# Linear attention and a gated MLP on one core: first loads, GpSimd's constants and the opening matmuls rearranged

## The chip, the core and the metric

The kernel runs on one core of one Trainium2 chip. The core has five engines that run their own instruction streams and wait for each other by semaphores: TensorE (PE in the profile; its weight loads are PEld), VectorE (DVE), ScalarE (ACT), GpSimd (POOL) and SyncE (SP). Transfers between HBM and SBUF run on 16 DMA engines that all queues share. The metric is the device time of one execution in microseconds. Before the change it is 287.11 us (median of 6 runs, 286.8 to 287.7).

## The reference

```python
kv = np.einsum('bhsd,bhse->bhde', k, v)                # 8 batches, 8 heads, 576 rows, 64 columns
out = np.einsum('bhsd,bhde->bhse', q, kv)
rms = np.sqrt(np.mean(out * out, axis=-1, keepdims=True) + 1e-06)
x = (out / rms * g_norm)                               # -> 4608 tokens x 512 (8 heads x 64)
h = x @ w_in                                           # 512 x 2048
g = h * (1.0 / (1.0 + np.exp(-1.702 * h)))
return g @ w_out                                       # 2048 x 512, fp32
```

All inputs are fp32. There is no softmax: each head's 64 x 64 `kv` is formed from all its rows, then multiplied by q, normed, and the result of all heads is the input row of the MLP.

## The kernel before

**Tiles.** Heads are taken in four pairs of two (128 columns). The MLP runs over nine tiles of 512 tokens: tile t below 8 holds the first 512 rows of batch t, and tile 8 holds the 64 remaining rows of all eight batches. For a tile the MLP first makes the hidden values in 16 column blocks `fo` of 128 (`hT`, L438: four matmuls over the row blocks `ko` of w_in, then a gate on ScalarE, L447, into `gT`), then projects them (`o`, L475: 4 output blocks `mo` times 16 `fo`). Row block `ko` of w_in meets exactly head pair `ko` of x, so a matmul with `ko` = 3 needs the attention result of pair 3.

**Order.** The schedule is manual: each engine gets its instructions in the order in which the program writes them, and waits for what each one needs. The attention of batch t+1 is woven into the MLP of tile t: `units1` are called after column block `fo` of the first half, `units2` after step n of the projection's 64 steps. The lists in the main loop (`at1`, `at2`) are these places.

**Casting loads.** All arithmetic is in fp16, so most fp32 inputs are cast while they are loaded, and all such loads are issued from GpSimd. Its instructions and its DMA issues are one stream in program order. A load waits at issue, where needed, for the landing of the eighth load before it.

**The start.** Batch 0 (`First`) has nothing to be woven into. Pair 0's k, q and v are loaded as fp32 from SP (L147) and cast by VectorE and ScalarE (L553 to L555). GpSimd first sets the constants: `ident` (L152, for the transposes of q) and `ones2` (L161 to L163: a block mask for `kv`, and the weights of the row sums `ss`), and then issues the casting loads of pairs 1 to 3 (q, k, v of each), with w_in's first row block for columns 0 to 511 put between q and k of pair 3, and then the rest of w_in in seven pieces. TensorE starts with 64 matmuls of 64 columns and 4 of 512 on zeros, so that its clock is up when the data comes; `busy(n)` are more of these. Each pair then goes through `q` (transposes, L393, copied to `qT` by VectorE), `kv` (L376, masked into `kvb` by VectorE, L383), `out` (L259, squared by ScalarE into `sq`, L279), `sums` (`ss` L339 on TensorE, `ln` L341 on ScalarE), `rs` (L347, ScalarE) and `apply` (L353, VectorE, which writes the pair's rows of `xT`). `ss` is `sums` and `rs` in one. The call list from L571 on interleaves pairs, and puts the first w_in matmuls (`d0.mm(ko, fo)`) between them: row block 0 before `kv(3)`, row blocks 1 and 2 after it, of six column blocks in all (GROUP), and row block 3 of the six at the end.

**Behind it.** After the w_in loads GpSimd issues w_out in pieces and batch 1's q, k and v among them. The remaining rows of batch 0 (`out(NPAIR)`, four matmuls of 64 columns at L270) are called after column block 7 of tile 0. PSUM is in three pools: `ps_h` (3 buffers), `ps_a` (3) and `ps_o` (2); a tile waits until the one that had its buffer has been read.

## Time and profile before

| quantity | value |
|---|---|
| median of 6 runs | 287.11 us |
| the profiled execution's own time | 287.02 us |
| its span, first to last instruction | 285.3 us |
| TensorE busy | 277.9 us, 97% |
| ScalarE, VectorE, GpSimd busy | 156.0, 118.9, 59.8 us |
| granted TensorE clock, mean | 0.999 |
| casting queue (software_dynamic), whole span | 15.59 MB written, 33.8% of 16 engines |

A line of the timeline is: start, length, engine, source line, operation, what it writes and reads, count, and in brackets how long the engine sat idle before and what ended that. A line of the chain that ended last is: start, length, what. A line of the table by stage is: stretch, its length, busy time (and instructions) of PE, PEld, DVE, ACT and POOL, the granted clock, the transfers' busy share and the GB/s that they moved (counted in bytes written, so a casting load reads twice as much). Matmuls overlap, so the length of one (379 ns for 512 columns) is longer than the distance from start to start (216 ns).

### The profile page before, as it was taken

The page shows a single profiled execution, that of the slowest core. Times are in us where ns is not written, and L with a number is a line of the kernel's source. Part 1 is how long each engine was busy: PE and PEld are TensorE (multiplying, and loading weights), DVE is VectorE, ACT ScalarE, POOL GpSimd, SP SyncE. Part 2 cuts the span into 40 slices and gives each one's busy share as a digit, 9 for nine tenths or more (in the row PEclk, how much of TensorE's full clock was granted, in tenths as well). Part 3 has the DMA queues.
Part 4 walks back from the last instruction along what each step waited for, and adds up shares of the span by engine and source line. Part 5 has one row for each costly group of instructions (what it writes and reads, how often), then busy time and mean ns, then how long its engine had stood idle before and what let it go on. Part 6 is the DMA issues. An engine that isn't in the chain of part 4 may idle for free.

```text
span 285.3 us, 4458 instructions
## 1 busy us (share of the span) xinstructions
PE 277.9 (97%) x1768; PEld 136.8 (48%) x1768; DVE 118.9 (42%) x230; ACT 156.0 (55%) x273; POOL 59.8 (21%) x86
## 2 busy tenths in 40 slices
PE   7799999999999999999999999999999999999995
PEld 5334554455445544554455445544454444444443
DVE  2550557527661657147713852286327400110001
ACT  2688439766575645574468536763666365016400
POOL 8762372111211121112011401130001100000000
PEclk9999999999999999999999999999999999999999
DMA  8999999998579356953798278925401410012022
GB/s 180 176 199 205 205 224 256 240 247 152 125 163 256 66 133 171 243 90 64 223 206 145 40 211 214 174 38 184 85 0 37 118 68 0 2 62 85 0 74 75
DMA packets 55158, 38.78 MB, mean 136 GB/s; under 512 B 31282, under 2 KB 52018, under 8 KB 55010
## 3 DMA queue, kind: packets, MB, share of 16 engines
q0 software_dynamic: 16048, 15.59, 33.8%
q1 hardware_dynamic: 38688, 22.39, 30.1%
q10 hardware_dynamic: 402, 0.52, 0.5%
q8 instruction: 14, 0.23, 0.3%
q14 instruction: 6, 0.05, 0.1%
HBM read 36.73 MB, written 9.44 MB: 162 GB/s over the span
## 4 chain that ended last, share of the span: by engine, by line
PE 93%; DMA 2%; POOL 2%; ACT 1%; DVE 0%; issue 0%
PE hT L438 43%; PE o L475 42%; PE kvp L227 3%; DMA vbuf<-in_v_dram 2%; PE outR L291 2%; PE oh L507 1%; PE ss L339 1%; POOL qraw L91 1%; POOL kraw L91 1%; POOL vbuf L91 0%; PE q L416 0%; ACT sq L279 0%; PE outT L270 0%; PE outT L259 0%; ACT ln L341 0%; ACT rs L347 0%
## 5 line engine op out<-in xcount | busy, mean ns | idle before, releaser
L475 PE MATMUL o<-w_out_sb,gT 128*128 128x512 f16 x560 | 130.7, 379 | 0.0
L447 ACT ACTIVATE gT<-hT 128x512 f16<-128x512 f32 x144 | 84.5, 601 | 75.9 <-PE hT L438 75.8
L438 PE MATMUL hT<-xT,w_in_sb 128*128 128x512 f16 x512 | 116.5, 379 | 1.2 <-DMA w_in_sb<-in_moe_w_in_dram 1.2
L438 PEld LDWEIGHTS <-w_in_sb 128*128 128x128 f16 x576 | 54.5, 98 | 63.6 <-DMA w_in_sb<-in_moe_w_in_dram 1.8
L475 PEld LDWEIGHTS <-gT 128*128 128x128 f16 x560 | 52.9, 98 | 56.7 <-issue 0.4
L485 DVE COPY osb<-o 128x512 f32<-128x512 f32 x20 | 13.8, 690 | 62.4 <-PE o L475 62.4
L323 POOL TENSOR_TENSOR x<-xr,g_all 128x512 f16<-128x512 f32 x12 | 15.3, 1272 | 70.4 <-DVE xr L316 46.3
L218 DVE COPY kpad<-kraw 64x576 f16<-64x576 f16 x56 | 25.0, 446 | 1.3
L240 DVE CAST kvb<-kvp 64x128 f16<-64x128 f32 x28 | 8.1, 289 | 39.9 <-PE kvp L227 39.7
L302 DVE TENSOR_REDUCE sum<-sq 128x8 f32<-128x512 f16 x24 | 15.8, 679 | 19.1 <-ACT sq L299 19.1
L112 POOL DMA_DIRECT2D kraw<-in_k_dram x16 | 10.0, 628 | 50.5 <-DVE kpad L218 34.6
L316 DVE TENSOR_TENSOR xr<-outR,sum 128x512 f32<-128x512 f32 x24 | 15.5, 686 | 11.1 <-ACT sum L313 11.1
L112 POOL DMA_DIRECT2D vbuf<-in_v_dram x16 | 9.7, 610 | 31.7 <-PE kvp L227 28.1
L323 DVE TENSOR_TENSOR x<-xr,g_all 128x512 f16<-128x512 f32 x12 | 15.2, 1267 | 0.7
L299 ACT ACTIVATE sq<-outR 128x512 f16<-128x512 f32 x24 | 13.6, 590 | 2.0 <-PE outR L291 1.6
L279 ACT ACTIVATE sq<-outT 128x512 f16<-128x512 f32 (+1 forms) x16 | 7.7, 486 | 12.5 <-PE outT L259 11.1
L227 PEld LDWEIGHTS <-kpad 128*128 128x128 f16 x252 | 11.1, 98 | 6.4
L438 PE MATMUL hT<-x_rem,w_in_sb 128*128 128x512 f16 x64 | 14.0, 379 | 0.0
L485 ACT COPY osb<-o 128x512 f32<-128x512 f32 x15 | 8.7, 582 | 6.3 <-PE o L475 6.3
L227 PE MATMUL kvp<-vbuf,kpad 128*128 128x64 f16 x252 | 11.9, 193 | 0.0
L312 ACT ACTIVATE sum<-sum,eps_t 128x16 f32<-128x16 f32 x12 | 3.7, 308 | 15.0 <-DVE sum L302 14.9
L341 ACT ACTIVATE ln<-ss,eps_t 128x512 f32<-128x512 f32 (+1 forms) x16 | 9.4, 586 | 3.2 <-PE ss L339 3.1
(64 smaller groups left out, 143.8 us busy)
## 6 DMA issues: line engine op xcount, KB each, us to landing
qf<-in_q_dram SPq DMA_DIRECT2D x5, 1024.0 KB, 9.4
out_dram<-osb SPq DMA_DIRECT2D x10, 512.0 KB, 2.9
kraw<-in_k_dram POOLq DMA_DIRECT2D x12, 288.0 KB, 7.5
vbuf<-in_v_dram POOLq DMA_DIRECT2D x12, 288.0 KB, 5.5
out_dram<-osb SPq DMA_DIRECT2D x6, 192.0 KB, 5.8
w_in_sb<-in_moe_w_in_dram POOLq DMA_DIRECT2D x4, 256.0 KB, 8.2
w_out_sb<-in_moe_w_out_dram POOLq DMA_DIRECT2D x2, 512.0 KB, 14.0
w_out_sb<-in_moe_w_out_dram POOLq DMA_DIRECT2D x4, 256.0 KB, 10.2
```

Of the source, the lines that this page charges most:

```text
L112: nc.gpsimd.dma_start(out=raw[n][l * PH : (l + 1) * PH, c0:c1, 0 : NH * D], in_=srcs[n][b].rearrange("(c l) (p j) d -> l p c (j d)", l=2, ...
L218: nc.vector.tensor_copy(out=kpad[r, c, :, l * D : (l + 1) * D], in_=kraw[r, c, 0 : NH * D].rearrange("p (j d) -> p j d", j=NH),)
L227: nc.tensor.matmul(self.kvp[:, c, :], kpad[:, c, j, :], vbuf[:, c, j * D : (j + 1) * D], start=(j == 0), stop=(j == NH - 1),)
L299: nc.scalar.activation(sq, t, AFT.Square)
L302: nc.vector.tensor_reduce(out=self.sum2[:, j % 2, :], in_=sq.rearrange("p (h d) -> p h d", h=H), op=ALU.add, axis=mybir.AxisListType.X,)
L316: nc.vector.tensor_mul(xr[:, i], self.o[j + i].rearrange("p (h d) -> p h d", h=H), s2[:, i, :].unsqueeze(2).to_broadcast([P, H, D]),)
L323: (nc.vector if i else nc.gpsimd).tensor_mul(self.x16[:, j + i, :].rearrange("p (h d) -> p h d", h=H), xr[:, i], g_all.unsqueeze(1).to_bro ...
L341: nc.scalar.activation(ln[:, 0:n], t[:, 0:n], AFT.Ln, bias=eps_t, scale=1.0 / D)
L438: nc.tensor.matmul(self.h[fo], w_in_sb[:, ko, fo * P : (fo + 1) * P], self.x[:, ko], start=(ko == 0), stop=(ko == KO - 1),)
L447: nc.scalar.activation(self.gT[:, fo, :], self.h[fo], AFT.Gelu_apprx_sigmoid)
L475: nc.tensor.matmul(os[mo], gT[:, fo, mo * P : (mo + 1) * P], w_out_sb[:, fo, :], start=(fo == 0), stop=(fo == FO - 1),)
L485: copy(osb[:, mo, :], os[mo])
```

## The change

1. v of pair 0 is no longer an fp32 load from SP with a cast on VectorE. It is the first casting load of GpSimd, ahead of everything else there.
2. GpSimd issues q, k, v of pair 1 and q of pair 2 before it sets `ident` and `ones2`. k and v of pair 2 and all of pair 3 follow.
3. w_in's first piece isn't put among pair 3's loads. After v of pair 3 come row blocks 0 and 1 in one load, then 2 and 3, then columns 4–5, 6–9 and 10–15: five loads instead of eight.
4. TensorE's opening is three fp32 matmuls of 512 columns on a new tile `zeros`, in place of 64 of 64 columns and 4 of 512.
5. In the call list, `kv(3)` and `out(3)` come before the first w_in matmul. The w_in matmuls then run in the order of `ko`: four column blocks each, `ss(3)` after the third of `ko` 0, and the column blocks 4 and 5 after all four of the first four.
6. The loads of w_out and of batch 1 are regrouped, batch 1's units sit at other steps, the order of column blocks at the head of tile 1 is 0, 1, 2, 3, batch 2's kv runs one column block sooner, and tile 7's output is stored in two halves.

```diff
     first = {}
-    for n in "kqv":
+    early_load("v", 0, 0, 1)
+    for n in "kq":
         first[n] = stage.tile([P, H, J * D], F32, name=f"{n}f", tag=f"{n}f")
...
+    zeros = const.tile([P, SM], F32)
+    nc.vector.memset(zeros, 0.0)
     nc.vector.memset(kvb[1], 0.0)
...
+    for n in "qkv":
+        early_load(n, 0, 1, 2)
+    early_load("q", 0, 2, 3)
     nc.gpsimd.affine_select(
...
-    for c in range(1, NPAIR):
-        for n in "qkv":
+    for c in range(2, NPAIR):
+        for n in "qkv"[c == 2 :]:
             early_load(n, 0, c, c + 1)
-            if c == NPAIR - 1 and n == "q":
-                load_w_in(0, 4, 0, 1)
-    load_w_in(0, 4, 1, 2)
+    load_w_in(0, 4, 0, 2)
     load_w_in(0, 4, 2, KO)
     load_w_in(4, GROUP)
-    load_w_in(GROUP, 8)
-    load_w_in(8, 10)
-    load_w_in(10, 13)
-    load_w_in(13, FO)
+    load_w_in(GROUP, 10)
+    load_w_in(10, FO)
...
-            order = [(ko, fo) for part in ((0, 3, 1, 2), range(4, group)) for ko in (0, 1) for fo in part]
+            order = [(ko, fo) for part in (range(4), range(4, group)) for ko in (0, 1) for fo in part]
...
-    nc.vector.tensor_copy(vbuf[0:PE_, 0, :], first["v"])
...
-    for _ in range(64):
-        nc.tensor.matmul(
-            idle_ps[:, 0:D], kvb[1][:, 0, :], kvb[1][:, 0, 0:D], start=True, stop=True
-        )
-    busy(4)
+    for _ in range(3):
+        nc.tensor.matmul(idle_ps, zeros[:, 0:P], zeros, start=True, stop=True)
...
     a0.q(3)
+    a0.kv(3)
+    a0.sums(2)
     a0.apply(1)
+    a0.out(3)
+    a0.rs(2)
+    a0.apply(2)
+    busy(1)
     d0 = Hidden(0)
-    d0.mm(0, 0)
-    a0.sums(2)
-    a0.rs(2)
-    d0.mm(0, 1)
-    d0.mm(0, 2)
-    d0.mm(0, 3, ps_a, "att")
-    a0.kv(3)
-    a0.apply(2)
-    a0.out(3)
     for fo in range(4):
-        d0.mm(1, fo)
+        d0.mm(0, fo, *((ps_h, "hT") if fo < 3 else (ps_a, "att")))
         if fo == 2:
             a0.ss(3)
             a0.apply(3)
-    for fo in range(4):
-        d0.mm(2, fo)
+    for ko in range(1, KO):
+        for fo in range(4):
+            d0.mm(ko, fo)
     for fo in range(4, GROUP):
-        for ko in range(KO - 1):
+        for ko in range(KO):
             d0.mm(ko, fo, ps_o, "o")
-    for fo in range(GROUP):
-        d0.mm(KO - 1, fo)
...
-    load_half("k", 1, 0, 2)
-    load_w_out(8, 10)
-    load_w_out(10, 12)
-    load_half("v", 1, 0, 2)
-    load_half("k", 1, 2, NPAIR)
-    load_half("v", 1, 2, NPAIR)
-    load_w_out(12, 14)
-    load_w_out(14, FO)
+    for c in (0, 2):
+        load_half("k", 1, c, c + 2)
+        load_half("v", 1, c, c + 2)
+        if c == 0:
+            load_w_out(8, 12)
+        else:
+            load_w_out(12, 14)
+            load_w_out(14, FO)
...
-    HALVED = (2, 3, 4, 5, 6)
+    HALVED = (2, 3, 4, 5, 6, 7)
...
-                at2((21, 21, 38, 38)[c], of(1, "pack_k", c))
-                at2((36, 37, 46, 47)[c], of(1, "kv", c))
-                o = (41, 43, 52, 53)[c]
+                at2((21, 21, 33, 33)[c], of(1, "pack_k", c))
+                at2((27, 28, 42, 43)[c], of(1, "kv", c))
+                o = (32, 35, 50, 53)[c]
                 at2(o, of(1, "out", c))
                 if c == NPAIR - 1:
-                    at2(48, load_kv, 2)
-                at2((45, 48, 56, 58)[c], of(1, "ss", c))
-                at2((48, 51, 56, 60)[c], of(1, "apply", c))
+                    at2(46, load_kv, 2)
+                at2((38, 46, 56, 59)[c], of(1, "ss", c))
+                at2((38, 46, 56, 59)[c], of(1, "apply", c))
...
-                at1(12 if t == 1 else f0, load_q, t + 2)
-                at1((11 if t == 1 else 9) + 4, load_kv, t + 2)
+                at1(f0, load_q, t + 2)
+                at1((10 if t == 1 else 9) + 4, load_kv, t + 2)
             for c in range(NPAIR):
                 at1(f0, of(b, "pack_k", c))
-                at1((11 if t == 1 else 9) + c, of(b, "kv", c))
+                at1((10 if t == 1 else 9) + c, of(b, "kv", c))
```

## The prediction

> **What bounds the kernel now.** I read the page first, then the chain that ended last in order of time, TensorE's timeline over the first 23 us, the waits, and the transfers' busy time by stage. From the page:
>
> ```profile
> span 285.3 us, 4458 instructions
> PE 277.9 (97%) x1768; PEld 136.8 (48%) x1768; DVE 118.9 (42%) x230; ACT 156.0 (55%) x273; POOL 59.8 (21%) x86
> PE 93%; DMA 2%; POOL 2%; ACT 1%; DVE 0%; issue 0%
> ```
>
> TensorE is the bound, and what is not TensorE (POOL, DMA) is the start. From start to start of TensorE's instructions, less their own length, I count about 5.2 us of holes between 5 and 18 us, and after 18 us one of 0.24 us (the `ss` at 45.95). So the body can give nothing but that 0.24; everything is decided before about 22 us. The chain there:
>
> ```profile
> 1.85 0.77 POOL qraw L91
> ...
> 7.75 6.82 DMA vbuf<-in_v_dram
> 14.61 0.40 PE kv L376 x12
> 15.04 0.30 DVE kvb L383
> 15.38 0.39 PE outT L259
> 15.77 0.65 PE hT L438 x3
> 16.46 0.38 PE ss L339
> 17.92 4.49 PE hT L438 x20
> 22.41 0.12 PE outT L270 x4
> ```
>
> POOL issues the casting loads, the last one of batch 0 (v of pair 3, below v3) lands at 14.57, and from 16.46 TensorE never stops again. The matmuls of the rest (`outT` L270, behind w_in's column block 7) start at 22.25. **I take that 22.25 as the mark: its shift is the shift of the end.** Just before:
>
> ```profile
> 13.18 0.39 PE L438 MATMUL hT<-xT,w_in_sb 128*128 128x512 f16 x1 [1.17 <-DMA w_in_sb<-in_moe_w_in_dram]
> 16.87 0.69 ACT L341 ACTIVATE ln<-ss,eps_t 128x512 f32<-128x512 f32 x1 [0.47 <-PE ss L339]
> 17.59 0.63 ACT L347 ACTIVATE rs<-ln 128x512 f32<-128x512 f32 x1
> 18.25 0.75 DVE L353 SCALAR_TENSOR_TENSOR xT<-outT,g_col,rs 128x512 f16<-128x512 f32 x1 [2.27 <-ACT rs L347]
> ```
>
> From pair 3's `ss` (16.46) to its `xT` (19.00) is 2.54 us. Before fills this with 12 matmuls at 0.216 us (2.6 us) that don't need pair 3, so the first one that does starts at 19.05 with no hole. The transfers by stage (the last two columns are their busy share and GB/s):
>
> ```profile
> 9.00:10.40 1.40, 1.14 (x14) 0.41 (x13) 0.53 (x3) 0.94 (x3) 1.21 (x2) 1.00 1.30 198
> 10.40:12.20 1.80, 1.47 (x26) 0.80 (x26) 1.55 (x4) 1.75 (x4) 1.75 (x3) 1.00 1.14 117
> 12.20:15.00 2.80, 1.63 (x17) 0.78 (x17) 1.07 (x2) 1.86 (x4) 1.58 (x3) 1.00 1.23 196
> ```
>
> The casting queue moves 200 GB/s (bytes written) from 5 to 48 us, a q, k or v load landing every 0.73 us and 256 KB of w_in every 1.32 us, except in one slow stretch: the first w_in load lands 1.99 us after the load ahead of it where 0.66 would do. That is 1.33 us lost, just where w_in is first read.
>
> **What the Trainium skill says.** *DMA: Bandwidth & Descriptors*, section "SWDGE vs HWDGE vs iDMA": only GpSimd-issued transfers may cast, so v of pair 0 (v0) must join that one queue. Its section "Anatomy of one DMA" gives about 2.0 us plus bytes/436 GB/s for one such transfer, as an estimate 2.7 us for 295 KB read. The trace shows 4.9 us for the first ones, so about 2 us of that is standing behind others. *SBUF — State Buffer*, section "SBUF: two separate sides": VectorE operations in a two-port mode keep GpSimd from writing descriptors; before's first issue (1.79) comes after VectorE's memsets (0.83 to 1.22), so the trace doesn't show it. *FP8 and Floating Point Precision*, section "TensorE Precision Notes": an fp32 matmul takes four passes.
>
> **The change part by part.**
>
> *v0 and the constants.* SP loses one issue (0.45 us) and VectorE one cast (0.56). POOL's first issue moves from 1.79 to about 0.78, when SP starts too. Before, the casting queue's first load landed 0.26 us after SP's last (6.67 and 6.41). SP's last is now q, at 5.22 before, so v0 lands near 5.5, and the stream starts 1.19 us sooner with 0.73 us more in it: −0.46 us net. `kv(0)` stood behind two dummies anyway (7.04, without the cast 6.95): 0.1 us, hidden in the wait for later pairs. The four constant instructions (1.02 to 1.85, 0.83 us) now stand behind five issues: 0.78 + 0.83 + 0.80 + 0.63 + 0.63 + 0.80 = 4.5, done by 5.3; `ident` is needed at 6.1 and `ones2` at 7.5. Behind them k2 is issued at 5.3. If nothing stood before it, it would need 2.7 (skill) to 3.6 us (v at 90.00 landed 4.23 us later, less the 0.7 us that its double size takes): 8.0 to 8.9. The stream itself delivers k2 at 5.5 + 5 x 0.73 = 9.2. So the pause is covered by 0.3 to 1.2 us; if k2 took 4.9 us from its issue like the first loads of before, it would land at 10.2, and all loads behind it up to 0.9 us later (bounds: 0 and +0.9; I take 0). The DVE lock could add some tenths to v0's issue, or nothing: I take nothing.
>
> *w_in not split.* Order now q3, k3, v3, then w_in rows 0–255. v3 lands at 5.5 + 9 x 0.73 = 12.1 (before 14.57). The first w_in lands with ko 0 and 1 together: before its second piece landed at 15.21, the same bytes now give 15.21 − 0.46 = 14.75 if the slow stretch stays with w_in, 13.4 without it. The larger later pieces (6–9, 10–15) land whole at about 20.0 and 23.95 (2.6 and 3.95 us for 2 and 3 times 256 KB), needed at about 20.6 and 24.2: covered by 0.25 to 0.6 us.
>
> *Pair 3 ahead of w_in.* `kv(3)` at 12.1, `outT` 0.77 us later (14.61 to 15.38 before) at 12.9, `sq` done at about 14.2 (ACT has `ln` 0.69 of pair 2 ahead), `rs(2)` to 14.8. But `ss(3)` is queued on TensorE behind three w_in matmuls. They wait for 14.8, so `ss(3)` starts at 14.8 + 3 x 0.216 = 15.45, and pair 3's `xT` is ready 2.58 us later, at 18.03. Behind `ss(3)` now only 9 matmuls need no pair 3 (before 11 and `ss` itself): 14.8 + 13 x 0.216 = 17.6. A new hole of 0.43 us. Then 4 + 8 + 8 matmuls of column blocks 0 to 7: 18.03 + 20 x 0.216 = 22.35. **Against 22.25: +0.1 us.** In before, the same late w_in cost less, because its four first matmuls ran while v3 was still coming.
>
> *Opening.* 3 fp32 matmuls are 3 x 4 x 512 = 6,144 columns; 64 x 64 + 4 x 512 is 6,144 too. They start after `zeros` (twice the 0.27 us of `kvb`'s memset) at about 1.55 instead of 1.27. Before went from 56 ns per 64 columns to 0.216 per 512 near 4.9 us, so they end near 5.9, ahead of 6.1: nothing. Wholly at the slow rate they end at 6.7; `kv(3)` has 0.7 us of waiting to absorb it.
>
> *Batch 1.* The same units at other steps. `kv(1)` of batch 1 comes at 36.9 while VectorE's `kpad` copies end at 36.96: +0.1. w_out 8–11 lands 1.4 us later than before's 36.59, at 37.6, needed at about 38. `ss(3)` at step 59 removes the 0.24 hole; hT's third block, now third in the order, waits for `ln` (to 47.73, TensorE there at 47.44): +0.15. Sum about 0. In tile 1 the kv blocks one w_in column block sooner wait for v landing at 56.24 against a need at 56.75: hidden by 0.5. t=7's halved store ends under 40 us of t=8: nothing.
>
> Sum: +0.1 in the head, +0.1 for semaphore hops, 0 behind: **+0.2 us**. The profiled execution took 287.02 us (span 285.3, so 1.7 around it), 0.09 under the median 287.11. Forecast 287.3, own range 286.9 to 287.7.
>
> **Rivals.**
>
> *The pause is not covered, or the slow stretch falls on k3 and v3 (slower).* With k2 late by 0.6 to 0.9 us, w_in's first piece lands near 15.4 to 15.6 and the mark at 15.6 + 0.65 + 2.58 + 4.3 = 23.1: +0.9, 288.0. It decides from about 0.5 us of lateness. For: before's loads all took 4.8 to 5.2 us, issue spacing 0.69 and landing spacing 0.73 are almost alike. Against: the later v load took 4.2 with twice the bytes.
>
> *The slow stretch goes (faster).* It came with w_in's first packets; if their place or their split made it, w_in lands at 13.4. Then `ss(3)` waits for `sq` to 14.2, `ln(3)` for ACT's `rs(2)` to 14.8, `xT` is ready at 16.9, the mark is 16.9 + 4.3 = 21.2: −1.0, 286.1. For: nothing like it is at w_out's first load. Against: six times within 0.9 us say it is in every run.
>
> *TensorE stays at its slow rate, or a late hole.* The skill's *TensorE: Matmul & The Clock Gate*, "Part 1", has the fast clock after some 3.4 us of sustained work; before agrees (1.27 to 4.9). If three fp32 matmuls don't count, or the waits at 12 to 15 us undo it, the 33 matmuls to the mark last 0.43 instead of 0.216 for up to 3.4 us: +1.5 to +2, 289.
>
> **How the numbers follow.** Chances: forecast 0.36, pause or stretch 0.32, stretch gone 0.20, slow clock or late hole 0.10, rest 0.02. What a measurement can tell from no change is 0.2%, 0.57 us. Slower by more: 0.08 of the forecast's, 0.26 of the second, all 0.10, 0.01: 0.45. Faster: 0.20. Within: 0.35. The range leaves out the clock case and the edge of the fast one: 286.0 to 288.6.
>
> **What would show it.** Right: v0 lands near 5.5, k2 with no gap behind q2, v3 near 12.1, first hT near 14.8, a hole of about 0.4 us before the first matmul on pair 3, mark near 22.4, no `ss` hole near 46. Wrong: the casting rate stays at 200 GB/s when w_in begins, or sags 0.5 us after q2, or 0.43 us matmuls after 6 us.

## The result, and the profile after

The changed kernel takes 288.9 us (median of 28 runs, 287.7 to 291.25) against 287.14 us before (median of 65 runs): ratio 1.0056, 95% interval 1.0042 to 1.007. (The ratios of this document are not the quotients of the medians: executions that lost clock weigh in them on both sides.) It is slower by 0.6%; the forecast was 287.3. The profiled execution took 288.91 us, its span is 287.1 us (before 287.02 and 285.3).

The granted clock differs from execution to execution: in 22 of 29 executions of the changed kernel TensorE's granted clock was halved for one or two stretches of 3.41 us after the start (their mean clock is below 0.9965), in the profiled one for one stretch, while all executions of before that the five groups of runs contain show this 40 times in 257. Where I write "at full clock", I mean the median of the executions without such a stretch: 288.26 us for the changed kernel, 286.93 to 287.07 for before in the five groups.

From the page of the changed kernel:

```profile
span 287.1 us, 4334 instructions
PE 281.0 (98%) x1707; PEld 135.5 (47%) x1707; DVE 119.0 (41%) x230; ACT 156.4 (54%) x273; POOL 57.9 (20%) x83
PE 94%; POOL 2%; DMA 2%; issue 0%; DVE 0%; POOLq 0%
```

TensorE is "busy" for 3.1 us more than before with 61 instructions fewer, so part of its work took longer (the clock, below). The mark of the prediction, the start of the remaining rows' `outT` (now L271), moved from 22.25 to 24.00, +1.75 us. From the mark to the end of the span it is 263.14 us, before 263.01. **All of the loss lies ahead of the mark.** The chain that ended last, of the changed kernel (start, length, what):

```profile
1.33 0.82 POOL vbuf L91
...
8.19 5.43 DMA vbuf<-in_v_dram
13.62 0.14 issue
13.75 0.40 PE kv L377 x12
14.15 0.02 issue
14.18 0.30 DVE kvb L384
14.48 0.04 issue
14.52 0.61 PE outT L260
15.13 0.43 PE idle L562
15.56 0.02 issue
15.57 1.46 PE hT L439 x3
17.04 0.43 PE ss L340
17.46 6.70 PE hT L439 x29
24.16 0.12 PE outT L271 x4
```

v of pair 3 (v3) lands at 13.62, not at 12.1; the first w_in piece at 15.53, not at 14.75. And `outT` needs 0.61 us where it had 0.39. The timeline of the changed kernel has the opening, GpSimd's first issue, and the place where the prediction put a hole of 0.43 us (start, length, engine, line, what, and in brackets the idle time before it):

```profile
1.54 5.49 PE L572 MATMUL idle<-zeros 128*128 128x512 f32 x6 [1.54 <-DVE zeros L153]
1.33 0.82 POOL L91 DMA_DIRECT2D vbuf<-in_v_dram  x1 [0.88 <-POOLq L710]
16.83 0.63 PE L340 MATMUL ss<-sq,ones 128*128 128x512 f16 x1
17.50 0.69 ACT L342 ACTIVATE ln<-ss,eps_t 128x512 f32<-128x512 f32 x1 [1.22 <-PE ss L340]
18.88 0.75 DVE L354 SCALAR_TENSOR_TENSOR xT<-outT,g_col,rs 128x512 f16<-128x512 f32 x1 [1.82 <-ACT rs L348]
```

The hole shrank to 0.15 us (ahead of the first pair-3 matmul at 19.69): `ss` and the first two of the nine w_in matmuls behind it took longer than at the full rate and filled part of it. Two tables by stage of the changed kernel show both losses (stretch, its length, busy time of PE, PEld, DVE, ACT and POOL, granted clock, the transfers' busy share, GB/s):

```profile
4.00:5.00 1.00, 1.00 (x2) 0.34 (x1) 0.67 (x1) 0.12 (x1) 0.92 (x3) 1.00 1.08 139
5.00:10.00 5.00, 5.00 (x60) 2.18 (x59) 0.90 (x4) 1.18 (x2) 4.90 (x11) 1.00 1.24 177
10.00:14.00 4.00, 2.91 (x56) 1.56 (x52) 2.52 (x6) 3.49 (x7) 3.62 (x6) 1.00 1.17 163
...
11.10:14.52 3.42, 2.45 (x51) 1.34 (x47) 2.30 (x6) 2.89 (x7) 3.04 (x5) 1.00 1.16 164
14.52:17.93 3.41, 3.39 (x8) 1.02 (x9) 1.36 (x2) 2.19 (x4) 1.28 (x3) 0.50 1.32 201
```

All queues together move 177 GB/s from 5 to 10 us and 163 from 10 to 14, where before had 200 outside its one slow stretch. And the clock is 0.50 from 14.52 to 17.93: matmuls stand 0.427 us apart instead of 0.216. How much is each? In the profiles below with the new order and a kept clock, the mark comes 7.6 to 7.8 us after the first w_in matmul (e17: 15.15 to 22.72). From 15.57 that gives 23.14: of the +1.75, 0.9 is late data and 0.86 the clock, in this execution.

### The profile page after: what moved, and what is told of

The parts are those of the page before. It is cut to its first block, busy times and chain, and to the rows that moved or that the text cites. A ratio compares the mean times of both kernels' runs of the same rounds, so it can differ in the third digit from the quotient of the medians.

```text
span 287.1 us, 4334 instructions
## 1 busy us (share of the span) xinstructions
PE 281.0 (98%) x1707; PEld 135.5 (47%) x1707; DVE 119.0 (41%) x230; ACT 156.4 (54%) x273; POOL 57.9 (20%) x83
## 4 chain that ended last, share of the span: by engine, by line
PE 94%; POOL 2%; DMA 2%; issue 0%; DVE 0%; POOLq 0%
PE hT L439 44%; PE o L476 42%; PE kvp L228 3%; DMA vbuf<-in_v_dram 2%; PE outR L292 2%; PE oh L508 1%; PE ss L340 1%; POOL vbuf L91 1%; POOL qraw L91 1%; POOL kraw L91 1%; PE outT L260 1%; PE q L417 0%; PE outT L271 0%; PE idle L562 0%; PE kv L377 0%
## 5 line engine op out<-in xcount | busy, mean ns | idle before, releaser
L324 POOL TENSOR_TENSOR x<-xr,g_all 128x512 f16<-128x512 f32 x12 | 15.3, 1271 | 70.1 <-DVE xr L317 52.1
L317 DVE TENSOR_TENSOR xr<-outR,sum 128x512 f32<-128x512 f32 x24 | 15.4, 686 | 11.1 <-ACT sum L314 11.1
## 6 DMA issues: line engine op xcount, KB each, us to landing
kraw<-in_k_dram POOLq DMA_DIRECT2D x12, 288.0 KB, 7.2
vbuf<-in_v_dram POOLq DMA_DIRECT2D x12, 288.0 KB, 5.4
```

Of the source, the lines that this page charges most:

```text
L317: nc.vector.tensor_mul(xr[:, i], self.o[j + i].rearrange("p (h d) -> p h d", h=H), s2[:, i, :].unsqueeze(2).to_broadcast([P, H, D]),)
L324: (nc.vector if i else nc.gpsimd).tensor_mul(self.x16[:, j + i, :].rearrange("p (h d) -> p h d", h=H), xr[:, i], g_all.unsqueeze(1).to_bro ...
```

## The experiments

The first theory that I stated was the order together with the clock (parts 3, 4 and 5: TensorE runs short of work while it waits for w_in, and then slowly), its rival the pause of the constants (part 2). After the first four runs a third joined: v of pair 0 (v0) in the casting queue (part 1). The table gathers what the changed kernel and the 18 others gave. "First issue", "w_in 1" (the first piece of w_in to be used) and "4–5" (w_in's columns 4 and 5) are GpSimd's first casting issue and the landings, of the profiled execution in us; "clock kept" counts executions without a halved stretch. The columns from "first issue" to "mark" are of one execution each, which need not be a typical one: e1's is the fastest of its seven (287.24 us), e8's the slowest of its 22 (288.98).

| kernel | median | ratio (95%) | first issue | v3 | w_in 1 | 4–5 | mark | clock kept | at full clock |
|---|---|---|---|---|---|---|---|---|---|
| changed | 288.9 | 1.0056 (1.0042–1.007) | 1.33 | 13.62 | 15.53 | 18.36 | 24.00 | 7/29 | 288.26 |
| e1 | 288.81 | 1.0058 (1.0036–1.008) | 1.31 | 13.00 | 14.81 | 17.39 | 22.43 | 2/7 | 287.94 |
| e2 | 290.09 | 1.0092 (1.006–1.0123) | 1.32 | 15.28 | | | 25.04 | 1/6 | 288.06 |
| e3 | 287.16 | 1.0006 (0.9992–1.0019) | 1.79 | 12.96 | 14.36 | 17.34 | 21.98 | 13/14 | 287.11 |
| e4 | 287.6 | 1.0021 (1.0005–1.0037) | 1.79 | 14.04 | | | 21.89 | 19/22 | 287.48 |
| e5 | 289.01 | 1.0062 (1.0044–1.0079) | 1.80 | 13.87 | 15.17 | 18.10 | 24.06 | 5/17 | 287.99 |
| e6 | 287.83 | 1.0036 (1.0016–1.0055) | 1.32 | 13.35 | 14.62 | 17.54 | 22.36 | 20/22 | 287.81 |
| e7 | 288.46 | 1.0052 (1.0032–1.0071) | 1.33 | 13.59 | 15.62 | 18.68 | 23.24 | 14/20 | 288.4 |
| e8 | 288.35 | 1.0027 (1.0008–1.0046) | 1.79 | 13.98 | 15.01 | 17.69 | 24.16 | 10/22 | 287.35 |
| e9 | 289.4 | 1.0066 (1.0044–1.0087) | 1.79 | 15.18 | | | 23.94 | 3/22 | 287.74 |
| e10 | 287.14 | 0.9982 (0.9964–0.9999) | 1.80 | 14.04 | | | 22.32 | 22/22 | 287.14 |
| e11 | 286.79 | 0.9987 (0.9973–1.0002) | 1.79 | 12.88 | 14.18 | 17.49 | 21.89 | 21/22 | 286.79 |
| e12 | 290.35 | 1.01 (1.0057–1.0144) | 3.55 | 15.00 | 17.02 | 20.00 | 25.48 | 0/4 | |
| e13 | 287.98 | 1.0018 (0.9995–1.004) | 1.79 | 13.59 | 14.86 | 18.06 | 22.60 | 8/12 | 287.61 |
| e14 | 287.0 | 0.9976 (0.9957–0.9995) | 1.80 | 12.82 | 14.24 | 17.79 | 22.08 | 19/20 | 286.99 |
| e15 | 288.78 | 1.0051 (1.0034–1.0068) | 1.79 | 13.96 | 15.26 | 18.09 | 22.98 | 7/20 | 287.97 |
| e16 | 286.75 | 0.9988 (0.9974–1.0001) | 1.79 | 12.86 | 14.18 | 17.25 | 21.87 | 21/22 | 286.75 |
| e17 | 288.64 | 1.0051 (1.0032–1.007) | 1.79 | 13.43 | 15.10 | 18.00 | 22.72 | 3/7 | 287.82 |
| e18 | 286.66 | 0.9978 (0.9966–0.9991) | 1.79 | 13.07 | 14.35 | 17.26 | 22.08 | 21/22 | 286.66 |

Where the w_in cells are empty, w_in comes in before's pieces, which don't compare (e2, e4, e9, e10).

### One part undone at a time

**e1**: the changed kernel with before's opening.

```diff
-    zeros = const.tile([P, SM], F32)
-    nc.vector.memset(zeros, 0.0)
...
-    for _ in range(3):
-        nc.tensor.matmul(idle_ps, zeros[:, 0:P], zeros, start=True, stop=True)
+    for _ in range(64):
+        nc.tensor.matmul(
+            idle_ps[:, 0:D], kvb[1][:, 0, :], kvb[1][:, 0, 0:D], start=True, stop=True
+        )
+    busy(4)
```

> The changed kernel with the opening of before (64 matmuls of 64 columns and 4 of 512, no zeros tile). Theory 1 (the changed kernel loses 1.75 us at the mark in two parts: w_in's first piece lands late and pair 3 stands behind it, +0.9 us; and TensorE's clock is halved for one window of 3.4 us from 14.5 us because TensorE waits too much between 11 and 14.5 us, +0.9 us): the opening is not the cause, the clock still drops in most executions, 288.4 to 289.0 us. Rival (the fp32 opening itself keeps the clock unsettled): clock 1.00 from about 5 us on without a drop, 288.0 to 288.3 us. Beside it: if VectorE's zeros memset held up GpSimd, v of pair 0 is now issued at 0.8 to 1.05 us instead of 1.33.

288.81 us: nothing comes back, and the clock was halved in 5 of 7 executions. The fp32 opening is not the cause. GpSimd's first issue stays at 1.31 although `zeros` is gone, so VectorE's memset of `zeros` isn't what holds it.

**e2**: the changed kernel with parts 3 and 5 undone.

```diff
-    load_w_in(0, 4, 0, 2)
+            if c == NPAIR - 1 and n == "q":
+                load_w_in(0, 4, 0, 1)
+    load_w_in(0, 4, 1, 2)
...
     a0.q(3)
+    a0.apply(1)
+    d0 = Hidden(0)
+    d0.mm(0, 0)
+    a0.sums(2)
...
     a0.kv(3)
-    a0.sums(2)
-    a0.apply(1)
+    a0.apply(2)
     a0.out(3)
...
```

> The changed kernel with w_in split among pair 3's loads and TensorE's call order as before (parts 3 and 5 undone; v of pair 0, the constants, the opening and the later parts stay changed). Theory 1: the first w_in matmuls again run while v of pair 3 is coming, so no whole window is poor in work and the clock stays up, and no hole before the first matmul on pair 3; the mark moves only by the lateness of v of pair 3 (0.2 to 1.0 us): 287.3 to 288.1 us. Rival (the casting queue's new head is what costs): most of the loss stays, 288.5 to 289 us.

290.09 us: no better than the changed kernel, if anything worse. The order alone is not the cause.

**e3**: the changed kernel with parts 1 and 2 undone, that is with before's loads up to pair 3 and GpSimd's constants first.

```diff
-    early_load("v", 0, 0, 1)
-    for n in "kq":
+    for n in "kqv":
...
-    for n in "qkv":
-        early_load(n, 0, 1, 2)
-    early_load("q", 0, 2, 3)
     nc.gpsimd.affine_select(
...
+    for n in "qkv":
+        early_load(n, 0, 1, 2)
+    early_load("q", 0, 2, 3)
...
+    nc.vector.tensor_copy(vbuf[0:PE_, 0, :], first["v"])
```

> The changed kernel with v of pair 0 loaded from SP and cast on VectorE and the constants ahead of all casting loads (parts 1 and 2 undone; order of w_in and of calls, opening and later parts stay changed). Theory 1: the order is what costs, so the loss mostly stays: v of pair 3 near 12.6 us, w_in's first piece at 14.5 to 15.3, clock drop in most executions: 288.2 to 289.0 us. Rival (the casting queue's new head costs): back to 287.1 to 287.6 us.

287.16 us, not to be told from before, with parts 3 to 6 still in. **The loss is in parts 1 and 2.** The same table by stage, of e3:

```profile
4.00:5.00 1.00, 1.00 (x3) 0.48 (x2) 0.67 (x1) 0.00 (x0) 1.00 (x2) 1.00 1.05 245
5.00:10.00 5.00, 4.07 (x60) 1.81 (x58) 1.92 (x6) 1.43 (x2) 4.49 (x8) 1.00 1.28 201
10.00:14.00 4.00, 3.10 (x53) 1.71 (x54) 2.38 (x7) 3.49 (x7) 3.51 (x6) 1.00 1.27 200
```

200 GB/s from 5 to 14 us, against 177 and 163. These are all queues together, and up to 6.96 us e3 still moves SP's third load. By queue (packets, MB, share of 16 engines), the stretch from 5 to 10 us of the changed kernel, then of e3:

```profile
q0 software_dynamic: 1247, 0.88, 124.4%
...
q0 software_dynamic: 1290, 0.92, 121.5%
q1 hardware_dynamic: 69, 0.08, 6.3%
```

So the casting queue by itself is only a little slower there; it doesn't take up what SP's third load left free. From 10 to 14 us no SP load of the start is under way in either, and the casting queue moves 163 against 200.

**e4**: before with part 6 alone (its lists of steps and its late loads).

```diff
...
-                at2((36, 37, 46, 47)[c], of(1, "kv", c))
-                o = (41, 43, 52, 53)[c]
+                at2((27, 28, 42, 43)[c], of(1, "kv", c))
+                o = (32, 35, 50, 53)[c]
...
-                at1((11 if t == 1 else 9) + c, of(b, "kv", c))
+                at1((10 if t == 1 else 9) + c, of(b, "kv", c))
```

> The kernel before with part 6 alone (loads of w_out and batch 1 regrouped, batch 1's units at other steps, order of column blocks at tile 1, batch 2 one block sooner, tile 7 stored in halves). Theory 1 and the prediction: the hole of 0.24 us at 45.95 goes, holes of about 0.1 us come at kv(1) and at hT's third block: 286.9 to 287.2 us, no change. Rival (the later parts carry some of the loss): 287.5 us or more.

287.6 us, 0.2% slower. The mark is no later than before (21.89), and behind it the trace has holes: 0.085 us at batch 1's `kv(1)`, 0.13 at hT's third block, as forecast, and 0.33 at 56.75, where batch 2's `kv` waits for a v that lands at 56.62. The forecast had that landing "hidden by 0.5". In the traces of the changed kernel and of e3, which have part 6 too, this hole isn't there (in e3 the v lands at 55.99 and `kv` starts at 56.45); what moved that landing is open.

### Parts 1 and 2 apart

**e5**: the changed kernel with its constants ahead of every casting load (part 2 undone).

```diff
-    early_load("v", 0, 0, 1)
     for n in "kq":
...
-    for n in "qkv":
-        early_load(n, 0, 1, 2)
-    early_load("q", 0, 2, 3)
     nc.gpsimd.affine_select(
...
+    early_load("v", 0, 0, 1)
+    for n in "qkv":
+        early_load(n, 0, 1, 2)
+    early_load("q", 0, 2, 3)
```

> The changed kernel with GpSimd's constants ahead of all casting loads again (part 2 alone undone; v of pair 0 stays first in the casting queue). Theory 2 (the 0.87 us in which GpSimd sets constants between the fifth and the sixth load isn't covered: the loads behind it land 0.9 to 1.6 us late, and the waits that this makes cost the clock a window as well): no gap between the landings of q of pair 2 and v of pair 2 beyond 0.75 us each, v of pair 3 near 12.6 to 13.1 us, clock 1.00 in most executions, 287.1 to 287.7 us. Rival (v of pair 0 in the casting queue is what costs, with 0.73 us more to carry): 288.2 to 288.9 us.

289.01 us: the loss stays, without the pause. The table by stage, of e5:

```profile
4.00:5.00 1.00, 1.00 (x2) 0.34 (x1) 0.27 (x1) 0.17 (x1) 1.00 (x2) 1.00 1.18 158
5.00:10.00 5.00, 5.00 (x60) 2.16 (x58) 0.87 (x4) 1.11 (x2) 4.70 (x8) 1.00 1.19 161
```

v0 lands at 5.75 here, but q of pair 1 only 1.70 us behind it, and q of pair 2 1.21 behind the load ahead of it, where 0.74 is regular.

**e6**: the changed kernel with v0 from SP (part 1 undone, the pause stays).

```diff
-    early_load("v", 0, 0, 1)
-    for n in "kq":
+    for n in "kqv":
...
+    nc.vector.tensor_copy(vbuf[0:PE_, 0, :], first["v"])
```

> The changed kernel with v of pair 0 loaded from SP and cast on VectorE again (part 1 alone undone; the constants stay in the middle of the loads, now behind the fourth casting load). Theory 2 (the pause costs): a gap of 0.9 to 2 us between two landings near 10 us stays, v of pair 3 at 13 to 14 us, clock drops in some executions, 288.2 to 289.2 us. Rival (v of pair 0 in the casting queue costs): 287.1 to 287.6 us.

287.83 us. The loads land at an even 0.74 us, also across the pause (q2 9.73, k2 10.46). Yet at full clock it is 0.70 us slower than e3 (287.81 and 287.11), which differs from it by the place of the constants alone. The traces put the lateness ahead of the pause: e6 issues its first casting load 0.47 us sooner than e3, but that load lands 0.42 us later (7.56 and 7.14), and v3 is 0.39 us later (13.35 and 12.96). So in this trace the pause itself was covered; what costs is something at the head. It is one trace each, and in the kernels that issue at 1.79 to 1.80 with three SP loads the first landing varies from 6.67 to 7.46, so why the first load lands late stays open.

**e7**: the changed kernel with filler matmuls in TensorE's waits (three ahead of `kv(3)`, three instead of one ahead of w_in).

```diff
     a0.q(3)
+    busy(3)
     a0.kv(3)
...
-    busy(1)
+    busy(3)
```

> The changed kernel with three dummy matmuls of 512 columns ahead of kv(3) and three instead of one ahead of the first w_in matmul, which run in TensorE's waits and are work that the output doesn't need. Theory 2 (a window of 3.4 us with too little TensorE work halves the clock for the next one): clock 1.00 from about 8 us on in nearly all executions, 0.5 to 0.9 us faster than the changed kernel, 287.9 to 288.4 us; the landings stay as they are. Rival (the clock drops for another reason, such as the opening): clock still 0.988 to 0.994 and 288.9 us.

The landings are as late as in the changed kernel (v3 13.59, w_in 15.62), but 14 of 20 executions keep their clock instead of 7 of 29, the median falls by 0.4 us to 288.46, and the mark of the profiled execution is 23.24, as worked out above for full clock. At full clock it is no faster (288.4 and 288.26). The table by stage of e7 for the two stretches that are 11.10 to 17.93 in the changed kernel:

```profile
11.10:14.52 3.42, 2.66 (x38) 1.13 (x32) 2.01 (x6) 2.42 (x6) 3.28 (x5) 1.00 1.13 142
14.52:17.93 3.41, 3.15 (x14) 1.10 (x15) 1.33 (x2) 2.79 (x5) 1.08 (x2) 1.00 1.31 199
```

**e8**: before with parts 3 and 5 alone.

```diff
-            if c == NPAIR - 1 and n == "q":
-                load_w_in(0, 4, 0, 1)
-    load_w_in(0, 4, 1, 2)
+    load_w_in(0, 4, 0, 2)
...
+    a0.kv(3)
+    a0.sums(2)
     a0.apply(1)
+    a0.out(3)
...
```

> The kernel before with the order of w_in and of TensorE's calls alone (parts 3 and 5; opening, v of pair 0, constants and later parts as before). Theory 2 (the order by itself is no loss, the mark was 21.98 us with it in the run with the old loads): mark 21.7 to 22.3 us, clock 1.00, 286.8 to 287.1 us. The prediction's step for the order (pair 3's chain behind w_in leaves a hole, +0.1 us and more): a hole of 0.2 to 0.45 us before the first matmul on pair 3, 287.1 to 287.4 us.

288.35 us in the median, 287.35 at full clock: 12 of 22 executions lose a stretch of clock. In the profiled execution v3 lands 1.67 us behind k3, so w_in comes at 15.01.

### Parts alone on the kernel before

**e9**: before with v0 as the first casting load, behind the constants (part 1 alone).

```diff
-    for n in "kqv":
+    for n in "kq":
...
+    early_load("v", 0, 0, 1)
     for c in range(1, NPAIR):
...
-    nc.vector.tensor_copy(vbuf[0:PE_, 0, :], first["v"])
```

> The kernel before with v of pair 0 as the first casting load, behind the constants (part 1 alone). Theory 3 (v of pair 0 in the casting queue starts that queue's packets while SP's k and q are still moving, and the queue then carries 130 to 195 GB/s from 5 to 14 us where it carries 200 with v on SP): rate from 5 to 10 us below 190 GB/s, loads of pair 3 about 1 us later, 0.8 to 1.5 us slower than before: 287.9 to 288.6 us. Rival (only the order of calls suffers from it, before's order hides it): 287.0 to 287.4 us.

289.4 us, ratio 1.0066. **Part 1 alone makes before slower by as much as the whole change does.** v2 lands 1.72 us behind k2, v3 at 15.18, and the clock is kept in 3 of 22.

**e10**: before with the fp32 opening alone (part 4).

```diff
+    zeros = const.tile([P, SM], F32)
+    nc.vector.memset(zeros, 0.0)
...
-    for _ in range(64):
...
+    for _ in range(3):
+        nc.tensor.matmul(idle_ps, zeros[:, 0:P], zeros, start=True, stop=True)
```

> The kernel before with the fp32 opening alone (part 4). Prediction's step: nothing, 287.0 to 287.3 us, clock 1.00 in nine of ten executions. Rival (the opening by itself moves the clock or the start): more than 0.3 us either way.

287.14 us; the clock is kept in all 22 executions, while before in the same group kept it in 47 of 59. At full clock it is no faster (287.14 against 287.01), so its ratio below 1 comes from the clock. How the opening does that wasn't found.

**e11**: before with parts 3, 4 and 5. Against e8:

```diff
+    zeros = const.tile([P, SM], F32)
+    nc.vector.memset(zeros, 0.0)
...
-    for _ in range(64):
...
+    for _ in range(3):
+        nc.tensor.matmul(idle_ps, zeros[:, 0:P], zeros, start=True, stop=True)
```

> The kernel before with order of w_in and calls and the fp32 opening (parts 3, 4, 5; v of pair 0 from SP, constants ahead of the loads, later parts as before). If the fp32 opening keeps the clock up in this order, as the run with parts 3 to 6 (13 of 14 executions at full clock) against that with parts 3 and 5 (10 of 22) suggests: clock 1.00 in most executions, 286.6 to 287.1 us, and perhaps faster than before. Rival (chance of the draw): half the executions with the clock halved for a window, 287.3 to 288.5 us.

286.79 us, 0.9987 (0.9973 to 1.0002): the order is worth something once the loads are on time, but not surely. 21 of 22 keep their clock, against e8's 10 of 22, and at full clock too e11 is 0.56 us faster than e8 (287.35). So in this order the opening, all that parts the two (they ran in different groups), is worth more than in e10; why is open.

**e12**: e5 with three memsets of a spare tile on GpSimd ahead of v0, so that the queue starts when SP's two loads are nearly done.

```diff
+    idle_g = const.tile([P, 4 * P], F32)
+    for _ in range(3):
+        nc.gpsimd.memset(idle_g, 0.0)
     early_load("v", 0, 0, 1)
```

> The run with the constants first and v of pair 0 first in the casting queue, and three memsets of a spare tile on GpSimd ahead of it (some 1.5 us that the output doesn't need), so that the first casting load is issued at about 3.3 us and moves after SP's two loads are done. Theory 3 (the overlap with SP's packets is what lowers the rate): 195 to 205 GB/s from 6 to 11 us; v of pair 0 lands near 7.5 us, all 0.5 to 1 us later than without the sag, 288.0 to 289.2 us. Rival (v of pair 0 being in that queue lowers the rate wherever it stands): 150 to 190 GB/s again.

290.35 us. The uneven landings stay: k1 comes at 9.82, 2.14 us behind q1, while SP's last load had landed at 4.94. So the gap needs no SP load under way beside it. The first issue is 1.75 us later than in e5, and columns 4–5 land 1.90 us later.

### What in part 1

Left open was why v0 in the casting queue costs so much: its place at the head, the number of casting loads, or SP's missing third load.

**e13**: e11 with one casting load more at the head, a second copy of v0 that nobody reads.

```diff
+    spare = stage.tile([P, 1, 2 * NJ * D], F16, name="spare", tag="spare")
+    nc.gpsimd.dma_start(
+        out=spare[0:PE_, :, 0 : 2 * NJ * D].rearrange("p c (l x) -> p (c l) x", l=2),
+        in_=early_src("v", 0, 0, 1),
+    )
     for c in range(1, NPAIR):
```

> Before with parts 3, 4 and 5 (as in e11), and one casting load more at the head of the casting queue: v of pair 0 a second time, into a spare tile that nobody reads. v of pair 0 itself still comes from SP. If one more casting load at the head makes the queue sag: over 1 us of excess landing gaps (over 0.74 a load) between the first landing and v of pair 3, which lands at 14.4 or later, and 288.3 us or more. If it is SP's missing third load that does it: no excess gap before v of pair 3, which lands 0.7 us later than in e11 (12.88), at 13.6; mark about 0.7 us later than e11's 21.89, 287.5 us.

No gap among the q, k and v loads, v3 at 13.59, the mark at 22.60 (e11: 21.89), and 287.61 us at full clock, as the branch for SP's missing third load had it: **one more casting load ahead of w_in costs 0.82 us** (e11: 286.79), its 0.7 us of transfer and a little more.

**e14**: v0 first in the casting queue, but v of pair 1 from SP in its place.

```diff
-        dst, src = first[n].rearrange("p (h x) -> p h x", h=2), early_src(n, 0, 0, 1)
+        dst, src = first[n].rearrange("p (h x) -> p h x", h=2), early_src(n, 0, int(n == "v"), 1 + int(n == "v"))
...
+    early_load("v", 0, 0, 1)
     for c in range(1, NPAIR):
-        for n in "qkv":
+        for n in "qk" if c == 1 else "qkv":
...
-    nc.vector.tensor_copy(vbuf[0:PE_, 0, :], first["v"])
+    nc.vector.tensor_copy(vbuf[0:PE_, 1, :], first["v"])
```

> As e11, but v of pair 0 is the first casting load and v of pair 1 comes from SP with VectorE's cast: nine casting loads and three from SP, as in e11. If the count of SP's loads or of casting loads decides: no excess gap among q, k and v, v of pair 3 near 12.9 as in e11, about 286.8 us. If v of pair 0 as the first casting load decides, whatever the counts: over 0.8 us of excess gaps before v of pair 3, which lands at 13.7 or later, 287.8 us or more.

287.0 us, v3 at 12.82, no gaps. v0's place at the head is harmless when nine casting loads and three SP loads remain.

**e15**: e5 with q of pair 1 ahead of v0.

```diff
-    early_load("v", 0, 0, 1)
-    for n in "qkv":
+    early_load("q", 0, 1, 2)
+    early_load("v", 0, 0, 1)
+    for n in "kv":
         early_load(n, 0, 1, 2)
```

> As e5 (the changed kernel with GpSimd's constants set first), but q of pair 1 is issued ahead of v of pair 0. If the place at the head decides: the excess gaps of e5 (0.97 behind v of pair 0, 0.48 at q of pair 2) go, v of pair 3 lands near 13.0 and the time is about 287.6 us. If the number of loads decides: excess gaps of over 1 us stay, v of pair 3 lands near 13.9, about 289 us.

288.78 us, 287.97 at full clock, as e5 (287.99). The gaps stay (v0 1.03 behind q1, k1 1.68 behind v0). Being first is not it. Nor is the number of casting loads by itself: e13 has ten as well, and no such gap. What e15 has and e13 hasn't is two loads from SP instead of three.

**e17**: e13 with SP's load of v0 taken away, so that v0 is used from the casting queue (before with parts 1, 3, 4 and 5).

```diff
-    for n in "kqv":
+    for n in "kq":
...
-    spare = stage.tile([P, 1, 2 * NJ * D], F16, name="spare", tag="spare")
-    nc.gpsimd.dma_start(
-        out=spare[0:PE_, :, 0 : 2 * NJ * D].rearrange("p c (l x) -> p (c l) x", l=2),
-        in_=early_src("v", 0, 0, 1),
-    )
+    early_load("v", 0, 0, 1)
...
-    nc.vector.tensor_copy(vbuf[0:PE_, 0, :], first["v"])
```

> Before with parts 1, 3, 4 and 5, which is e13 with v of pair 0 not loaded by SP as well: ten casting loads with the same first issue, two loads from SP. If the earlier start of the stream is worth what it shows (first landing 1.2 to 1.4 us before e13's 7.16): v of pair 3 near 12.4, columns 4 and 5 of w_in near 16.9, 286.9 us in executions at full clock. If the shorter SP queue only moves the slow stretch forward and the gain is lost: over 0.8 us of excess gaps among q, k and v, v of pair 3 at 13.6 or later, columns 4 and 5 of w_in near 18.1 as in e13 (18.06), 287.6 to 287.8 us at full clock (e13 287.61), and a clock window lost in more of the executions than e13's 4 of 12.

This pair is the cleanest. The chain, first of e13, then of e17:

```profile
1.79 5.36 DMA spare<-in_v_dram
...
9.43 7.75 DMA w_in_sb<-in_moe_w_in_dram
17.18 0.05 issue
17.23 1.04 PE hT L441 x4
18.27 0.02 issue
18.29 4.48 PE hT L441 x20
22.76 0.12 PE outT L273 x4
```

```profile
8.20 6.90 DMA w_in_sb<-in_moe_w_in_dram
15.10 0.05 issue
15.15 0.82 PE hT L437 x3
15.97 0.23 PE ss L338
...
17.60 0.76 DVE xT L352
18.36 0.04 issue
18.40 4.48 PE hT L437 x20
22.88 0.12 PE outT L269 x4
```

In e13 the first casting load lands at 7.16, in e17 at 5.73. And the 20 matmuls that lead to the mark start at 18.29 and at 18.40. The lead of 1.43 us at the start of the stream is gone by then: in e17 v of pair 1 comes 1.74 us behind k of pair 1 and w_in 1.67 behind v3, in e13 the loads are even up to w_in's first piece and the second one comes 2.32 us behind it. Columns 4–5 land at 18.06 and 18.00. At full clock it is 287.61 us (8 executions) and 287.82 (3): the earlier start brought no gain, and whether it cost anything three executions don't tell.

So the end of the stream doesn't follow its first landing. Read over the fifteen kernels whose loads can be compared (those with w_in cells in the table), the time from GpSimd's first issue to the landing of columns 4–5 falls into groups: nine casting loads 15.46 to 15.99 us (e3, e8, e11, e14, e16, e18), ten 16.21 to 16.45 (e5, e12, e13, e15, e17, of which e12 starts 1.75 us later than e5), and with the constants in the midst of the loads 16.22 for nine (e6) and 16.08, 17.03 and 17.35 for ten (e1, changed, e7). The gaps sort in another way. Leaving out those at a piece of w_in, all nine kernels with two loads from SP have a gap of 1.10 us or more among the q, k and v landings (1.10 to 2.14 at the largest); of the eleven with three, before among them, ten have none over 0.85, and e8 has its 1.67. Both were seen after the runs, on one trace each; what sets the pace, and what the slow stretches are, stays open.

### The versions the runs point to

**e16** is e11, **e18** is e14, each with pair 3's `ss` of batch 1 one step later, as part 6 has it.

```diff
-                at2((45, 48, 56, 58)[c], of(1, "ss", c))
+                at2((45, 48, 56, 59)[c], of(1, "ss", c))
```

> e11 (before with parts 3, 4 and 5) and one unit moved: pair 3's row sums of batch 1 at step 59 instead of 58, as part 6 has it. If the 0.24-us hole that e11 still has there goes and nothing else comes: 286.55 us, ratio 0.998, interval below 1. If a clock window is lost in part of the executions after all: 287 or more.

> e14 (v of pair 0 first in the casting queue, v of pair 1 from SP, parts 3, 4 and 5) with pair 3's row sums of batch 1 at step 59. If the 0.24-us hole goes and the head stays as in e14: 286.75 us and an interval below 1. If not: 287.0 us, no difference from before.

e16: 286.75 us, 0.9988 (0.9974 to 1.0001). e18: 286.66 us, 0.9978 (0.9966 to 0.9991), **faster than both kernels**, by 0.22% of before (0.09 to 0.34). At full clock the difference is 0.4 us (286.66, and 287.07 for before in the same group). Of the 0.24-us hole nothing is left over 0.1 us. Its timeline ahead of the mark:

```profile
13.21 0.38 PE L375 MATMUL kv<-vbuf,kraw 96*64 96x64 f16 x12 [0.69 <-DMA vbuf<-in_v_dram]
14.42 0.81 PE L437 MATMUL hT<-xT,w_in_sb 128*128 128x512 f16 x3
15.17 0.38 PE L338 MATMUL ss<-sq,ones 128*128 128x512 f16 x1
15.38 2.12 PE L437 MATMUL hT<-xT,w_in_sb 128*128 128x512 f16 x9
17.77 4.48 PE L437 MATMUL hT<-xT,w_in_sb 128*128 128x512 f16 x20 [0.27 <-DVE xT L352]
```

The first matmul on pair 3 still comes 0.43 us late behind `xT`; that hole is what the new order leaves on the table.

## Why the prediction was wrong

**The step that failed** is "SP's last is now q, at 5.22 before, so v0 lands near 5.5, and the stream starts 1.19 us sooner with 0.73 us more in it: −0.46 us net." The landing came later than that (6.25 here), but in e7 with the same loads it was 5.47, and the 0.73 was right. Wrong was to credit the earlier landing to everything behind it. e13 and e17 show that a lead of 1.43 us at the head is worth nothing at w_in. Part 1 doesn't bring w_in 0.46 us sooner but 0.92 us later (e17 15.10, e11 14.18). In time at full clock it costs 1.03 us (e17 against e11): 0.82 for the tenth load (e13 against e11), and for the shorter SP queue, instead of a gain, 0.2, which can't be told from nothing. With it fell "the casting queue moves 200 GB/s": that was before's rate (up to 6.41 us with SP's loads in it), and in the changed kernel slow stretches stand among the q, k and v loads as well as at w_in. Why the stream slows down when SP has one load less stays open.

**The first issue at 0.78** came at 1.33. GpSimd idles 0.88 us behind a wait of its own queue; e1 shows that `zeros` isn't the cause, and what is stays open. I had taken VectorE's end as the only thing ahead of it.

**The pause, "covered by 0.3 to 1.2 us"**: at k2 it was covered (10.29, 0.75 behind q2; in e6 0.73). k2 landed 4.6 us behind its issue at 5.68, nearer to the 4.9 of the first loads than to the 2.7 to 3.6 taken. (The upper bound was also reckoned short: 10.2 less 9.2 is 1.0, not 0.9.) Still, moving the constants cost 0.70 us with v0 from SP (e6 against e3). The traces show 0.42 of it as a later first landing, which the prediction didn't have. On top of part 1 it is 0.27 (changed against e5 at full clock, seven and five executions), which isn't clear of noise.

**The rivals.** The slower rival, "the pause is not covered, or the slow stretch falls on k3 and v3", had w_in at 15.4 to 15.6, the mark at 23.1 and 288.0 us. w_in came at 15.53, the mark at full clock is 23.1 to 23.2, and the full-clock median is 288.26. Its numbers were right, in part by luck, since its first mechanism (k2 late) was not; its second, a slow stretch ahead of w_in, is near what the traces show, though the changed kernel has it at q1 and v2 (1.08 and 1.10 us behind the load ahead) and not at k3 and v3. The faster rival, that the slow stretch goes, was wrong: in the changed kernel the gaps over the regular ones add up to about 2.1 us by w_in's second piece, against before's 1.33.

**The clock** was the rival with a chance of 0.10, as "the waits at 12 to 15 us undo it". The mechanism was right, with the matmuls of 0.43 us that were to show it, and came on top of the other in 22 of 29 executions; e7, which fills the waits and leaves the landings late, shows that the waits bring it. Its price is 0.65 us in the median (288.9 against 288.26), 0.86 in the profiled one, not 1.5 to 2, because for the first 1.05 us of the halved stretch (14.52 to 15.57) the w_in matmuls couldn't have started at the full clock either, as w_in landed at 15.53, and 0.28 us came out of the hole. It goes with the lateness of w_in: with the new order, the clock is kept in 95 of 100 executions where the first piece landed by 14.4 in the trace (e3, e11, e14, e16, e18), in 20 of 22 at 14.62 (e6), 8 of 12 at 14.86 (e13), 25 of 66 at 15.0 to 15.3 (e5, e8, e15, e17), 7 of 29 at 15.53 (changed). e7's fillers lift 15.62 to 14 of 20. e1 (14.81, 2 of 7) falls out of line, but its profiled execution, the fastest, is one of the two that kept the clock. All kernels at 14.4 or sooner have the fp32 opening, so a share of the opening, which parts e8 from e11, can't be ruled out. I should have asked of each term of lateness whether it also empties a stretch of TensorE's clock.

**What held.** The hole of 0.43 us before the first matmul on pair 3: 0.43 in e18, e6 and e15 (17.77, 18.05, 18.66). The 4.32 us from there to the mark: 4.31 in e18. The opening as nothing, on the kernel before: e10 is 0.9982 (0.9964 to 0.9999) by the clock, and no faster at full clock; with the new order it was worth more (e11 against e8). It ended between 5.8 (e3, e11) and 7.0 us (the changed kernel), against 5.9 and, "wholly at the slow rate", 6.7. The rest behind the mark at about 0: 263.14 against 263.01, with 0.085, 0.13 and the 0.24 that went, though part 6 by itself costs 0.2% (e4). w_out 8–11 landed at 38.09 and left no hole (36.59 and 1.4 make 38.0, not the 37.6 of the forecast).

The full-clock medians make a chain from before (286.98) to the changed kernel: parts 3 to 5 −0.19 (e11, 286.79), part 1 +1.03 (e17, 287.82), part 6 +0.17 (e5, 287.99), part 2 +0.27 (288.26), and the clock +0.65 (288.9). The kernels ran in several groups, whose full-clock medians of before differ by up to 0.14, and e17, e5 and the changed kernel have only three, five and seven executions at full clock, so of these terms only part 1's and the clock's are clear of noise.

## What to carry to other kernels

An earlier first landing is not an earlier stream: cost a load that moves into a queue as its full transfer time for everything behind it, and give credit for an earlier start only where a trace shows that the last load, not the first, comes sooner. Where TensorE is the bound, look at the waits that precede its first long run of matmuls: 0.9 us of late data cost another 0.65 us in the median, because the clock fell. If a load has to come sooner, take another one out of the queue in exchange (e14, e18) rather than adding to it.

## What the runs showed of the hardware

- The Trainium skill, *TensorE: Matmul & The Clock Gate*, "Part 1", section "What's actually happening", has a free-running window of 3413 ns and the lower clock after a whole idle window. The traces agree on the window: halved stretches are 3.41 us long, one or two in a row, and begin a multiple of 3.41 us after the clock first rose. They agree on free-running too: in the fifteen kernels with the fp32 opening TensorE starts at 1.53 or 1.54, and the clock rises anywhere from 4.42 (e11) to 7.76 (e5). So a window lies differently over the waits from one execution to the next; that this makes one execution keep its clock and the next lose it was not shown. They differ on idleness: in the changed kernel TensorE was busy for 2.45 us of the 3.42 ahead of the halved stretch. In the profiles the halved stretches followed windows with 1.39 to 2.45 us of busy time (e12, e9, e8, e5, e2, changed), and no window at full clock with 2.50 (e17) or more was followed by one. But before's window from 11.76 to 15.17 has 1.89, one of e8's has 2.32, one of e4's 2.38, and all three kept the clock behind them, so busy time alone doesn't decide.
- Three fp32 matmuls of 512 columns show as six entries and took 5.49 us in the changed kernel, where the clock rose only behind them (7.69). 16-bit ones of the same size stand 0.427 us apart at half the clock: about a quarter of the 1.8 us that each fp32 one took.
- Casting loads of 144 KB landed between 0.46 and 2.14 us apart at the start of the kernels with ten of them, though they were mostly issued 0.62 us apart. The landings of w_in's columns 6–9 and 10–15 are even again: 2.3 to 2.6 and 3.7 us behind the load ahead of them (the fifteen kernels with w_in cells in the table).
